# Two heads side by side on halves of the tensor array in float32, in place of one block-diagonal float32r product per pair of heads

## The chip, the cores and the metric

One core of a Trainium2 chip runs the kernel: TensorE for matrix products (PE, with PEld for the loading of its weights), VectorE (DVE), ScalarE (ACT), GpSimd (POOL), and SyncE (SP), which issues the DMAs. The metric is the device time of one execution in microseconds; lower is better. Float32r is a float32 format of which TensorE uses fewer bits in a product, and float32 is its full format, which the trace shows as two PE instructions for one product.

## The reference

A linear attention with a decaying state, and then a gated MLP over its output (4 batches, 8 heads, 768 tokens, 48 values a head; 384 channels, hidden size 1536):

```python
for t in range(S):
    kt, vt, rt = (k[:, :, t], v[:, :, t], r[:, :, t])
    cur = np.einsum('bhd,bhe->bhde', u[None] * kt, vt)
    y[:, :, t] = np.einsum('bhd,bhde->bhe', rt, state + cur)
    state = w[None, :, :, None] * state + np.einsum('bhd,bhe->bhde', kt, vt)
...
x = np.ascontiguousarray(attn_out.transpose(0, 2, 1, 3)).reshape(B, S, H * D)
xt = x.transpose(0, 2, 1)
h = xt @ U @ V
u = x + h.transpose(0, 2, 1)
ch = np.maximum(u @ w_ch1, 0.0) @ w_ch2
return (u + ch).astype(np.float32)
```

`w_ch1`, `w_ch2`, `U` and `V` arrive as float64, whose bits the kernel turns into float32 itself.

## The kernel before

The attention goes by chunks of 128 tokens, numbered `n` from 0 to 23, six to a batch. Tables of powers of w turn the decay into plain products within a chunk. Heads are taken in four pairs (`NP`), and a pair's 2 x 48 = 96 values (`PD`) lie on 96 partitions. For a chunk:

- `a_pre` makes on POOL `ks` (k scaled, for the state) and `dv` (the diagonal term; its sum over a head's values, `dg`, is DVE's).
- `a_tr_r` and `a_tr_k` give r and k with values on partitions, scaled by the tables (`rT`, `kT`). For chunks 0 to 5 PE transposes; from chunk 6 on DVE transposes 32 x 32 blocks (`bl`) that small DMAs bring from memory, and POOL multiplies by the table.
- The scores of the two heads of a pair come from one product: `kT` of the pair holds both heads on 96 partitions, and r is laid out block-diagonally, 128 columns with the first head's rows only and 128 with the second's. `bm`, a mask by partition, makes these halves. From chunk 6 on r and k are split into float32r high and low parts (`rh`, `rl`, `kh`, `kl`, on ACT and DVE), and three float32r products per pair (lines 388 to 390) make up one of nearly full precision. Chunks 0 to 5 (`plain`) use one float32 product per pair (line 383).
- `am`, the causal mask on the scores, is DVE's (three times ACT's and POOL's).
- `a_sq` reads the state: `rT` of a pair times `S`, whose 96 x 96 blocks are block-diagonal (line 410). `a_av` adds `am` times v, head by head (line 421), in the same PSUM bank (`pav`). `x` is that plus `dv` (line 430).
- `a_su` makes the state's update, `ks` of a pair times v of the pair, of which the two diagonal blocks count (line 449), and DVE and POOL form the next `S` (lines 457 and 458).

The MLP of a batch (`m_1`, `m_2`) is made of 48 steps over halves of the tokens and blocks of the hidden size; each step has 9 float32r products of 384 columns in `m_1` (lines 613 to 615) and 9 in `m_2` (631 to 633), with a ReLU and a split on ACT and DVE between them (`hh`, `hl`). The program runs the first batch's attention together with the conversion of the first 12 units of weights (`raw_w`, three DVE operations each, then ACT and POOL: the first stage), and then for each batch its MLP with the next batch's attention spread over it. A scheduler with a timeline of its own sets the order of instructions on each engine; each engine then works through its list in order. `queued` holds some weight conversions behind given steps.

Eight PSUM banks are shared by tags: `tr`, `sc`, `av` one each, `mm` two, `acc` three.

Of the kernel before, what the change touches and what calls it, by code (L numbers as in the profile page):

```python
# [23 lines left out]
def rwkv_moe(ctx: ExitStack, tc: tile.TileContext, r, k, v, w, u, U, V, w1, w2, out):  # L24
# [5 lines left out]
    PD = 2 * D  # L30
# [21 lines left out]
    def f32(ap):  # L52
        return ap.bitcast(F32)

# [7 lines left out]
    bm = const.tile([PD, 2, D], F32, name="bm")  # L62
    nc.gpsimd.memset(bm, 1.0)
    nc.gpsimd.affine_select(out=bm[:, 0, :], in_=bm[:, 0, :], pattern=[[0, D]], compare_op=ALU.is_gt,
                            fill=0.0, base=D, channel_multiplier=-1)
    nc.gpsimd.affine_select(out=bm[:, 1, :], in_=bm[:, 1, :], pattern=[[0, D]], compare_op=ALU.is_ge,
                            fill=0.0, base=-D, channel_multiplier=1)
# [11 lines left out]
    nc.sync.dma_start(wT[:, :, 0], w.rearrange("(q j) d -> (j d) q", j=2))  # L79
    ub = const.tile([128, H, D], F32, name="ub")  # L80

    def tables():
        """Powers of w by products of its repeated squares, and of their inverses."""
# [23 lines left out]
        for x_, t in ((1, tab), (0, tabr)):  # L107
            pt = ps_tile("tr", f"pt_tab{x_}", 1)
            for q in range(NP):
                nc.tensor.transpose(pt[:, q * PD:(q + 1) * PD], tabT[:, x_, q, :], ident[:PD, :PD])  # L110
            nc.scalar.copy(t, pt[:, :DM])
        w2p = const.tile([PD, NP, 1], F32, name="w2p")
        nc.vector.tensor_mul(w2p, top[0], top[0])
        nc.gpsimd.tensor_mul(wm, bm.rearrange("p j e -> p (j e)").unsqueeze(1).broadcast_to([PD, NP, PD]),
                             w2p.broadcast_to([PD, NP, PD]))

    def flags():
        """Whether any of w lies where the tables cannot serve."""
# [11 lines left out]
    wm = const.tile([PD, NP, PD], F32, name="wm")  # L130
# [4 lines left out]
    # One pool of equal slots: a unit of weights as it arrives, its two halves for the rest of the program,  # L135
    # and later the blocks of r and k.
# [27 lines left out]
    def unit(name, shape, parts, split):  # L164
        """Loads an array of float32 or of float64 (as its bits); gives float32 to be split into float32r halves."""
# [70 lines left out]
    NB = B * NCH  # L236
    loaded = {}
    pre = {}
# [11 lines left out]
    def a_load(n):  # L250
        b, c = divmod(n, NCH)
        ts = []
        if n < 4:
            t3 = xpool.tile([128, 3, H, D], F32, tag="uTl" if n % 2 else "uTh", name=f"ld_{n}", bufs=2)
            ts = [t3[:, i] for i in range(3)]
            for t, src in zip(ts, (r, k, v)):
                nc.sync.dma_start(t, src[b, :, c * C:(c + 1) * C, :].rearrange("h p d -> p h d"))
            loaded[n] = ts
            return
        for nm, src in (("r", r), ("k", k), ("v", v)):  # L260
            t = work.tile([128, H, D], F32, tag="ldv" if nm == "v" else "ldrk", name=f"ld{nm}_{n}", bufs=3 if nm == "v" else NRK)
# [4 lines left out]
    def a_load_blocks(n, i, q):  # L266
        # partitions 32 g + tt, free (pair, token block, i): 32 x 32 blocks of three chunks' tokens by (head, dim)
        b, c = divmod(n, NCH)
        if q == 0:
            bls[n, i] = big([PD, 2, 12, 32], F32, f"bl_{n}_{i}")  # L270
        t = bls[n, i]
        src = (r, k)[i % 2]
        for g, i0, j, d0, ln in ((0, 0, 0, 0, 32), (1, 0, 0, 32, 16), (1, 16, 1, 0, 16), (2, 0, 1, 16, 32)):
            sv = src[b, 2 * (2 * (i // 2) + q) + j, c * C:(c + 3) * C, d0:d0 + ln].rearrange("(m t) d -> t m d", t=32)
            nc.sync.dma_start(t[32 * g:32 * g + 32, q, :, i0:i0 + ln], sv)  # L275
# [3 lines left out]
    def fl(t):  # L279
        return t.rearrange("p h d -> p (h d)")  # L280
# [622 lines left out]
```

## Time and profile before

| | us |
|---|---|
| median of 3 runs | 495.33 (494.27 to 496.04) |
| the profiled execution, first to last instruction | 492.1 |
| PE busy | 461.5 |
| DVE busy | 303.3 |
| POOL busy | 235.6 |
| ACT busy | 149.6 |
| first MLP product starts at | 76.2 |

The profile is of one execution; the median of the runs is 3.2 us above its span. Busy time of PE counts overlapping instructions once, and its matmuls are pipelined, so a busy PE is not a PE at its best pace: that is read from the distances between the starts of its instructions. What ends an idle stretch is given behind an arrow with its line. All times in tables of stretches are counted from the span's start.

### The profile page before, as it was taken

The page shows a single profiled execution, that of the slowest core. Times are in us where ns is not written, and L with a number is a line of the kernel's source. Part 1 is how long each engine was busy: PE and PEld are TensorE (multiplying, and loading weights), DVE is VectorE, ACT ScalarE, POOL GpSimd, SP SyncE. Part 2 cuts the span into 40 slices and gives each one's busy share as a digit, 9 for nine tenths or more (in the row PEclk, how much of TensorE's full clock was granted, in tenths as well). Part 3 has the DMA queues.
Part 4 walks back from the last instruction along what each step waited for, and adds up shares of the span by engine and source line. Part 5 has one row for each costly group of instructions (what it writes and reads, how often), then busy time and mean ns, then how long its engine had stood idle before and what let it go on. Part 6 is the DMA issues. An engine that isn't in the chain of part 4 may idle for free.

```text
span 492.1 us, 7932 instructions
## 1 busy us (share of the span) xinstructions
PE 461.5 (94%) x2891; PEld 446.6 (91%) x2891; DVE 303.3 (62%) x543; ACT 149.6 (30%) x290; POOL 235.6 (48%) x227
## 2 busy tenths in 40 slices
PE   7869878979999999999999999999999999999994
PEld 6858757969998989999999999999999999999994
DVE  7998968997788666837677453676672533213112
ACT  3535524434332232333222322323231222211110
POOL 5957565747978571645777602468751021000000
PEclk9977969999999999999999999999999999999998
DMA  9999704554764663676267225542001152001001
GB/s 159 200 312 405 160 17 73 89 82 74 103 113 95 101 102 90 152 107 97 50 96 140 54 66 108 107 75 50 2 0 49 57 113 73 0 1 48 1 0 55
DMA packets 196880, 45.23 MB, mean 92 GB/s; under 512 B 187682, under 2 KB 193571, under 8 KB 196835
## 3 DMA queue, kind: packets, MB, share of 16 engines
q1 hardware_dynamic: 196834, 44.66, 44.2%
q8 instruction: 25, 0.41, 0.4%
q14 instruction: 21, 0.16, 0.1%
HBM read 35.79 MB, written 8.85 MB: 91 GB/s over the span
## 4 chain that ended last, share of the span: by engine, by line
PE 64%; DVE 14%; POOL 7%; issue 6%; SPq 4%; DMA 3%; ACT 1%; DVEq 0%; POOLq 0%; ACTq 0%
PE p L631 8%; PE p L632 8%; PE p L613 8%; PE p L633 8%; PE p L615 8%; PE p L614 8%; PE pav L421 5%; SPq L275 3%; DVE rl L353 2%; PE pav L410 2%; DVE raw_w L189 2%; POOL kT L323 2%; PE psu L449 2%; DVE raw_w L188 1%; POOL dv L295 1%
## 5 line engine op out<-in xcount | busy, mean ns | idle before, releaser
L619 DVE SCALAR_TENSOR_TENSOR hl<-p,hh 128x384 fp32r<-128x384 f32 x96 | 52.6, 549 | 102.1 <-ACT hh L618 102.0
L613 PE MATMUL p<-uTh,w1s 128*128 128x384 f32 x288 | 98.3, 344 | 2.8 <-DVE hl L619 2.5
L631 PE MATMUL p<-w2s,hh 128*128 128x384 f32 x288 | 98.5, 342 | 1.4 <-ACT hh L618 1.4
L614 PE MATMUL p<-uTl,w1s 128*128 128x384 f32 x288 | 97.7, 339 | 1.2 <-DVE uTl L546 1.2
L615 PE MATMUL p<-uTh,w1s 128*128 128x384 f32 x288 | 97.3, 338 | 0.0
L632 PE MATMUL p<-w2s,hh 128*128 128x384 f32 x288 | 96.7, 336 | 0.0
L618 ACT ACTIVATE hh<-p 128x384 fp32r<-128x384 f32 x96 | 46.7, 489 | 148.5 <-PE p L615 147.3
L633 PE MATMUL p<-w2s,hl 128*128 128x384 f32 x288 | 78.8, 338 | 0.1
L613 PEld LDWEIGHTS p<-uTh,w1s 128*128 128x128 f32 x288 | 54.4, 189 | 4.6 <-DVE hl L619 3.7
L631 PEld LDWEIGHTS p<-w2s,hh 128*128 128x128 f32 x288 | 54.2, 188 | 2.6 <-ACT hh L618 2.4
L614 PEld LDWEIGHTS p<-uTl,w1s 128*128 128x128 f32 x288 | 54.6, 190 | 2.0 <-DVE uTl L546 2.0
L615 PEld LDWEIGHTS p<-uTh,w1s 128*128 128x128 f32 x288 | 54.5, 189 | 0.0
L632 PEld LDWEIGHTS p<-w2s,hh 128*128 128x128 f32 x288 | 54.2, 188 | 0.0
L601 POOL TENSOR_TENSOR uTl<-ut,uTh 128x384 fp32r<-128x384 f32 x21 | 21.5, 1025 | 66.6 <-ACT uTh L600 65.2
L633 PEld LDWEIGHTS p<-w2s,hl 128*128 128x128 f32 x288 | 52.5, 189 | 0.5 <-DVE hl L619 0.2
L323 POOL TENSOR_TENSOR kT<-kT,tabT 96x512 f32<-96x512 f32 x18 | 27.3, 1518 | 42.0 <-DVE kT L321 32.7
L421 PEld LDWEIGHTS pav<-ldv,am 128*128 128x128 f32 x320 | 43.4, 198 | 1.5 <-DVE am L397 1.5
L421 PE MATMUL pav<-ldv,am 128*128 128x48 f32 x320 | 42.8, 272 | 0.6 <-DVE am L397 0.5
L397 DVE TENSOR_TENSOR am<-psc,mask 128x512 f32<-128x512 f32 x45 | 30.5, 678 | 9.7 <-PE psc L390 8.0
L353 DVE SCALAR_TENSOR_TENSOR rl<-rT,bm,rh 96x512 fp32r<-96x512 f32 x36 | 34.1, 959 | 3.9 <-ACT rh L351 3.9
L351 ACT ACTIVATE rh<-rT,bm 96x512 fp32r<-96x512 f32 x36 | 24.1, 716 | 22.8 <-POOL rT L323 22.6
L323 POOL TENSOR_TENSOR rT<-rT,tabT 96x512 f32<-96x512 f32 x18 | 24.8, 1379 | 10.8 <-DVE rT L321 10.7
(142 smaller groups left out, 766.6 us busy)
## 6 DMA issues: line engine op xcount, KB each, us to landing
raw_w<-in_moe_w_ch_dram SPq DMA_DIRECT2D x24, 384.0 KB, 7.8
out_dram<-x SPq DMA_DIRECT2D x24, 192.0 KB, 2.1
ud<-x SPq DMA_DIRECT2D x21, 192.0 KB, 2.0
ub<-ud SPq DMA_DIRECT2D x84, 48.0 KB, 2.3
ldr<-in_r_dram SPq DMA_DIRECT2D x20, 192.0 KB, 3.2
ldk<-in_k_dram SPq DMA_DIRECT2D x20, 192.0 KB, 4.0
ldv<-in_v_dram SPq DMA_DIRECT2D x20, 192.0 KB, 3.1
bl<-in_r_dram SPq DMA_DIRECT2D x48, 48.0 KB, 2.4
```

The lines of the kernel that those rows point to most:

```text
L323: nc.gpsimd.tensor_mul(xT, xT, tabT[:, i])
L353: nc.vector.scalar_tensor_tensor(rl[:, :, j, :], rT, bm[:, j, 0:1], f32(rh[:, :, j, :]), ALU.mult, ALU.subtract)
L397: nc.vector.tensor_tensor(am, pt.rearrange("p (h t) -> p h t", h=4), mask.unsqueeze(1).broadcast_to([128, 4, C]), ALU.mult)
L421: nc.tensor.matmul(avp[n][:, h * D:(h + 1) * D], lhsT=am[:, hh, :], rhs=vt[:, h, :], start=(c == 0 and h == 0), stop=(h == H - 1), skip_gr ...
L613: nc.tensor.matmul(pt, lhsT=wt[:, 0, fs], rhs=uh[:, ct, :], start=(ct == 0), stop=False)
L614: nc.tensor.matmul(pt, lhsT=wt[:, 0, fs], rhs=ul[:, ct, :], start=False, stop=False)
L615: nc.tensor.matmul(pt, lhsT=wt[:, 1, fs], rhs=uh[:, ct, :], start=False, stop=(ct == NCT - 1))
L618: i_hh = nc.scalar.activation(hh, pt, AF.Relu)
L619: i_hl = nc.vector.scalar_tensor_tensor(hl, pt, 0.0, f32(hh), ALU.max, ALU.subtract)
L631: nc.tensor.matmul(pt, lhsT=hh[:, ts_], rhs=W2[f][:, 0], start=(f == 0), stop=False)
L632: nc.tensor.matmul(pt, lhsT=hh[:, ts_], rhs=W2[f][:, 1], start=False, stop=False)
L633: nc.tensor.matmul(pt, lhsT=hl[:, ts_], rhs=W2[f][:, 0], start=False, stop=(f == NFT - 1))
```

## The change

Each head of a pair gets 64 partitions (`HP`), 48 of them used, so that the second head starts at partition 64. Scores are then two products per pair, one for each head, with 48 rows that lie in the upper or the lower half of the array (64 x 128); the state is kept as one 48 x 48 block per head at partitions 0 and 64, and its read is two products on these halves too. The update is two products whose 64 and 48 weight columns go to the left and the right half of the array (128 x 64). All of them are plain float32, for all chunks. `in_turn` fixes the order so that the halves alternate. `bm`, the block-diagonal layouts and the splits into high and low parts are gone.

```diff
-    PD = 2 * D
+    HP = 64
+    PD = HP + D
+    PE_ = 2 * HP
...
-        if plain(n):
-            rf = work.tile([PD, NP, 2, C], F32, tag="bd_rl" if odd else "bd_r", name=f"rf_{n}", bufs=1)
-            for j in range(2):
-                nc.scalar.activation(rf[:, :, j, :], rT, AF.Copy, scale=bm[:, j, 0:1])
...
-        for j in range(2):
-            nc.scalar.activation(rh[:, :, j, :], rT, AF.Copy, scale=bm[:, j, 0:1])
-        for j in range(2):
-            nc.vector.scalar_tensor_tensor(rl[:, :, j, :], rT, bm[:, j, 0:1], f32(rh[:, :, j, :]),
-                                           ALU.mult, ALU.subtract)
+        rT = work.tile([PE_, NP, C], F32, tag="rT", name=f"rT_{n}", bufs=2)
+        a_tr(n, 0, rT)
+        trs[n] = [rT]
...
-        nc.scalar.copy(kh, kT)
-        nc.vector.tensor_tensor(kl, kT, f32(kh), ALU.subtract)
...
+    def in_turn(steps):
+        last = None
+        for f in steps:
+            with ExitStack() as st:
+                if last is not None:
+                    st.enter_context(tc.issue_after(last.ins))
+                last = f()
...
-            nc.tensor.matmul(o, lhsT=kh[:, q, :], rhs=a, start=True, stop=False)
-            nc.tensor.matmul(o, lhsT=kh[:, q, :], rhs=bb, start=False, stop=False)
-            nc.tensor.matmul(o, lhsT=kl[:, q, :], rhs=a, start=False, stop=True)
+        pts = [ps_tile(tag, f"psc_{n}_{j}", 1) for j, tag in enumerate(("sc", "tr"))]
+        def one(q, j):
+            rows = head_rows(j)
+            return nc.tensor.matmul(pts[j][:, q * C:(q + 1) * C], lhsT=kT[rows, q, :], rhs=rT[rows, q, :],
+                                    start=True, stop=True)
+        in_turn([lambda q=q, j=j: one(q, j) for q in range(NP) for j in range(2)])
...
+            avp[n] = [ps_tile("av", f"pav_{n}_0", 1), ps_tile("sc", f"pav_{n}_1", 1)]
+        def one(q, j):
+            rows = head_rows(j)
+            return nc.tensor.matmul(avp[n][j][:, q * D:(q + 1) * D], lhsT=rT[rows, q, :], rhs=St[n][rows, q, :],
+                                    start=(q == 0), stop=False, skip_group_check=True)
...
-            nc.tensor.matmul(pt[:PD, q * PD:(q + 1) * PD], lhsT=ks[:, q * PD:(q + 1) * PD],
-                             rhs=vt[:, 2 * q:2 * q + 2, :].rearrange("p h d -> p (h d)"),
+            m = D if j else HP
+            k0 = (2 * q + j) * (HP if n < NCH else D)
+            return nc.tensor.matmul(pt[j * HP:j * HP + m, q * D:(q + 1) * D],
+                                    lhsT=ks.rearrange("p h d -> p (h d)")[:, k0:k0 + m], rhs=vt[:, 2 * q + j, :],
```

Further edits: a half of the heads (even or odd, `j`) now has its own score bank (`sc`, `tr`) and its own output bank (`av`; for the other `sc` from chunk 6 on, `mm` before), so `x` is written in two halves; r, k and `ks` of the first batch are padded to 64 values a head by small memsets on DVE; w is loaded by two DMAs; the block DMAs bring 64 instead of 48 values a head (four DMAs as before); `wm`, `S` and the sum of the state have half the columns; the slow path for other w takes its two buffers elsewhere.

The scheduler gives another order. Names carry the chunk's number first (`psc_13_1` is chunk 13's scores, odd heads) and then a running number. PE around chunk 13, beside the third batch's MLP, before; the rows left out are the MLP's, and more of the score products:

```order
L388 MATMUL psc_13_1_2312<-rh_13_2194,kh_13_2225 128x256
L389 MATMUL psc_13_1_2312<-rl_13_2195,kh_13_2225 128x256
L390 MATMUL psc_13_1_2312<-rh_13_2194,kl_13_2226 128x256
...
L410 MATMUL pav_13_2342<-S_12_2252,rT_13_2190 128x96 x4
...
L421 MATMUL pav_13_2342<-ldv_13_1753,am_13_0_2310 128x48 x4
...
L421 MATMUL pav_13_2342<-ldv_13_1753,am_13_1_2319 128x48 x4
...
L388 MATMUL psc_14_0_2458<-rh_14_2351,kh_14_2395 128x256
```

The same place in the change:

```order
L411 MATMUL pav_13_0_2355<-S_12_2270,rT_13_2212 128x48
...
L379 MATMUL psc_13_0_2320<-rT_13_2212,kT_13_2243 128x128
L379 MATMUL psc_13_1_2321<-rT_13_2212,kT_13_2243 128x128
...
L411 MATMUL pav_13_1_2356<-S_12_2270,rT_13_2212 128x48
L411 MATMUL pav_13_0_2355<-S_12_2270,rT_13_2212 128x48
...
L424 MATMUL pav_13_0_2355<-ldv_13_1786,am_13_0_2330 128x48 x4
L461 MATMUL psu_13_2413<-ldv_13_1786,ks_13_2183 64x48
L461 MATMUL psu_13_2413<-ldv_13_1786,ks_13_2183 48x48
...
L424 MATMUL pav_13_1_2356<-ldv_13_1786,am_13_1_2332 128x48 x4
...
L379 MATMUL psc_14_0_2471<-rT_14_2365,kT_14_2409 128x128
```

The eight scores now stand together, then 23 MLP products, then the rest of the state's read, both `pav` groups and the update in one piece, then 23 MLP products up to the next chunk's scores; only one product of the read stands apart, near the scores.

POOL at the end of the first stage, before: the states after chunks 3 and 4 (`S_3`, `S_4`), a mask's select, and weights (`w1s`, `w2s`).

```order
L458 TENSOR_TENSOR S_3_548<-S_3_548,wm_86 96x384
L394 AFFINE_SELECT am_4_0_567<-am_4_0_567 128x512
L201 TENSOR_TENSOR w2s_1_555<-raw_w2_1_234,w2s_1_555 128x384
L201 TENSOR_TENSOR w2s_2_589<-raw_w2_2_236,w2s_2_589 128x384
L458 TENSOR_TENSOR S_4_623<-S_4_623,wm_86 96x384
```

In the change:

```order
L471 TENSOR_TENSOR S_3_594<-S_3_594,wm_83 112x192
L311 TENSOR_TENSOR ks_6_964<-ldk_6_831,tab_84 128x384
L314 TENSOR_TENSOR dv_6_966<-ldr_6_829,ldk_6_831 128x384
L317 TENSOR_TENSOR dv_6_966<-dv_6_966,ub_80 128x384
L389 AFFINE_SELECT am_4_0_619<-am_4_0_619 128x512
L320 TENSOR_TENSOR dv_6_966<-ldv_6_833,dg_6_969 128x384
L311 TENSOR_TENSOR ks_7_1061<-ldk_7_837,tab_84 128x384
L314 TENSOR_TENSOR dv_7_1063<-ldr_7_835,ldk_7_837 128x384
L317 TENSOR_TENSOR dv_7_1063<-dv_7_1063,ub_80 128x384
L471 TENSOR_TENSOR S_4_681<-S_4_681,wm_83 112x192
```

The weights of this place moved ahead of `S_3`, and what chunks 6 and 7 need from POOL, which in before follows the first stage, moved between the two states.

DVE at the same place, before: the masks and the outputs `x` of chunks 4 and 5, with the last steps of three weight units between.

```order
L430 TENSOR_TENSOR x_4_637<-pav_4_592,dv_4_503 128x384
L190 SCALAR_TENSOR_TENSOR raw_w2_3_244<-raw_w2_3_244 128x384
L397 TENSOR_TENSOR am_5_0_642<-psc_5_0_639,mask_72 128x512
L190 SCALAR_TENSOR_TENSOR raw_w2_4_246<-raw_w2_4_246 128x384
L397 TENSOR_TENSOR am_5_1_653<-psc_5_1_650,mask_72 128x512
L190 SCALAR_TENSOR_TENSOR raw_w2_5_248<-raw_w2_5_248 128x384
L430 TENSOR_TENSOR x_5_689<-pav_5_666,dv_5_578 128x384
```

In the change, from the last step of the same weight unit on:

```order
L191 SCALAR_TENSOR_TENSOR raw_w2_5_249<-raw_w2_5_249 128x384
L392 TENSOR_TENSOR am_3_0_533<-psc_3_0_523,mask_72 128x512
L392 TENSOR_TENSOR am_3_1_535<-psc_3_1_524,mask_72 128x512
L434 TENSOR_TENSOR x_3_576<-pav_3_0_555,dv_3_462 128x4x48
L470 TENSOR_TENSOR S_3_594<-psu_3_585,S_2_515 112x192
...
L392 TENSOR_TENSOR am_4_1_622<-psc_4_1_610,mask_72 128x512
L319 TENSOR_REDUCE dg_6_969<-dv_6_966 128x8
L319 TENSOR_REDUCE dg_7_1066<-dv_7_1063 128x8
L434 TENSOR_TENSOR x_4_663<-pav_4_0_642,dv_4_541 128x4x48
L470 TENSOR_TENSOR S_4_681<-psu_4_672,S_3_594 112x192
...
L434 TENSOR_TENSOR x_5_741<-pav_5_1_728,dv_5_628 128x4x48
```

The weight units of the first stage now stand ahead of chunk 3's masks, and the sums `dg` of chunks 6 and 7 ahead of the state after chunk 4.

More of the change, by code (lines that the diff above doesn't have):

```diff
@@ L393, in a_sc, with a_am @@
+    def a_am(n, j):
+        pt = scs[n][j]
+        am = work.tile([128, 4, C], F32, tag="am", name=f"am_{n}_{j}", bufs=2)
+        if n < NCH and (n * 2 + j) % 4 < 1:
             nc.scalar.copy(am, pt.rearrange("p (h t) -> p h t", h=4))
```

181 lines of the change are left out of this document (83 added, 98 removed).

## The prediction

> **What bounds the kernel now.** I read the page's busy shares first, then busy times by stretch, then PE's timeline.
>
> ```profile
> PE 461.5 (94%) x2891; PEld 446.6 (91%) x2891; DVE 303.3 (62%) x543; ACT 149.6 (30%) x290; POOL 235.6 (48%) x227
> 0.00:77.00 77.00, 62.29 (x362) 54.16 (x362) 64.71 (x115) 34.35 (x68) 53.20 (x62) 0.84 0.78 200
> 77.00:175.00 98.00, 90.67 (x578) 86.55 (x579) 80.34 (x140) 34.63 (x69) 67.90 (x61) 0.98 0.60 96
> 175.00:285.00 110.00, 108.18 (x712) 106.47 (x712) 72.47 (x134) 33.42 (x62) 64.61 (x60) 1.00 0.53 96
> 285.00:384.00 99.00, 99.00 (x661) 98.39 (x661) 56.62 (x102) 27.59 (x53) 43.78 (x40) 1.00 0.27 57
> 384.00:492.00 108.00, 101.37 (x585) 101.05 (x583) 29.16 (x55) 19.63 (x41) 6.10 (x6) 0.98 0.15 40
> ```
>
> The columns are the stretch, its length, the busy time of PE, PEld, DVE, ACT and POOL, and the granted clock, DMA share and GB/s. Until 77 us the first batch's attention and the first weights run, with DVE the fullest engine (64.7 of 77). From 77 us the MLPs run with the other batches' attention in between, and PE is the bound: 7.3 us idle until 175, 1.8 until 285, none after. So three things count: what the new products cost on PE, what waits disappear before 285 us, and whether the first stage gets longer.
>
> Busy time hides PE's pace, since matmuls overlap. The pace is the distance between starts:
>
> ```profile
> 326.00 0.84 PE L449 MATMUL psu<-ldv,ks 128*96 128x96 f32 x8
> 326.68 1.02 PE L421 MATMUL pav<-ldv,am 128*128 128x48 f32 x8
> 327.52 0.42 PE L613 MATMUL p<-uTh,w1s 128*128 128x384 f32 x1
> 327.78 0.34 PE L614 MATMUL p<-uTl,w1s 128*128 128x384 f32 x1
> 327.95 0.34 PE L615 MATMUL p<-uTh,w1s 128*128 128x384 f32 x1
> 328.13 0.34 PE L613 MATMUL p<-uTh,w1s 128*128 128x384 f32 x1
> ...
> 332.00 1.03 PE L410 MATMUL pav<-S,rT 96*128 96x96 f32 x8
> 332.81 0.42 PE L613 MATMUL p<-uTh,w1s 128*128 128x384 f32 x1
> ...
> 334.81 0.28 PE L388 MATMUL psc<-rh,kh 96*128 96x256 f32 x1
> 334.93 0.28 PE L389 MATMUL psc<-rl,kh 96*128 96x256 f32 x1
> ...
> 335.52 0.99 PE L421 MATMUL pav<-ldv,am 128*128 128x48 f32 x8
> 24.19 1.96 PE L383 MATMUL psc<-rf,kf 96*128 96x256 f32 x8
> 25.99 0.60 PE L312 MATMUL ptr<-ident,ld 128*96 128x128 f32 x4
> ```
>
> An MLP product takes 0.174. The six score products from 334.81 to 335.52 take 0.118 each. Every float32 product is two PE instructions (x8 for four products): the state's read (L410) takes 0.81/8 = 0.101 each with 96 columns moving, the scores' times v (L421) 0.84/8 = 0.105 with only 48. So the moving side does not set this pace; it does at 256 columns (L383, first batch: 1.80/8 = 0.225), so that 128 columns cost at most 0.113, and I take 0.107. The update (L449), 96 weight columns instead of 128, takes 0.68/8 = 0.085: the pace goes with the weights' columns. The Trainium skill ("TensorE: Matmul & The Clock Gate", LDWEIGHTS) gives columns/1.2 ns, 107 for 128 and 80 for 96, and the trace agrees. And the MLP product behind a float32 group starts 0.26 before its successor instead of 0.174: leaving such a group costs 0.085.
>
> PE from 76.2 to 485.0 is 408.8 us. 1728 MLP products at 0.1735 are 299.8; 216 score products at 0.119 25.7; 15 state reads at 0.81 12.2; 36 halves of L421 at 0.84 30.2; 15 updates at 0.68 10.2; about 60 exits at 0.085 5.1; 36 G products 6.3 and 23 gate products 4.1 at 0.175. That is 393.6, so some 15 us are waits. The ends, and the PE waits that the profile names before 175 us:
>
> ```profile
> 76.21 0.44 PE L613 MATMUL p<-uTh,w1s 128*128 128x384 f32 x1
> 485.05 1.49 DVE L636 TENSOR_TENSOR x<-p,x 128x384 f32<-128x384 f32 x3 [1.69 <-PE p L633]
> PE p L613 <- DVE hl L619: 2.2, 2, 1.6
> PE psc L389 <- DVE rl L353: 1.6, 2, 1.2
> PE ph L524 <- DVE x L525: 1.5, 1, 1.5
> PE p L631 <- ACT hh L618: 1.4, 2, 0.9
> ```
>
> **The change on PE, per chunk beside an MLP.** Everything becomes float32 with 128 weight columns, except the update. Scores: 12 products become 8 (16 instructions, N=128). State read: 4 become 8 (16 instructions, N=48). L421 stays at 16. Update: 4 become 8, 16 instructions of 64 and 48 columns; from 0.105 at 128 and 0.085 at 96 the line gives about 0.065 and 0.055. No row of before shows products on halves of the array, so both ends are bounded. *Side by side*, a pair costs one: scores 8 x 0.107 = 0.86, state read 1.05 (its first product stands alone, behind the scores, then seven in four slots of 0.21), update about 0.5. *One after the other*: 1.71, 1.68, 0.95. Over 18 chunks (15 for read and update), before 25.7 + 12.2 + 10.2 = 48.1; side by side 15.4 + 15.8 + 7.5 = 38.7, or 9.4 less; one after the other 30.8 + 25.2 + 14.3 = 70.3, or 22 more. I take the first end: the halves have their own rows, or their own columns, of the array, and the order alternates them. Nothing measured here excludes the other.
>
> Between full array and halves there are some seven changes per chunk (into the scores and out, into the read, to L421, to the update, to L421, out), against some 3.5 float32 exits before. I price each like the only exit the trace has, 0.085: 18 x 3.5 x 0.085 = 5.4 more. Bounds: nothing, and 0.2 each (+20). The Trainium skill ("TensorEngine Tiling (Array Packing)", Key Properties) says that changing the tiling mode drains the engine; it gives no time and no run here shows it. PE's net: -9.4 + 5.4 = **-4**, between -15 and +11.
>
> **DVE, ACT, POOL.**
>
> ```profile
> L353 DVE SCALAR_TENSOR_TENSOR rl<-rT,bm,rh 96x512 fp32r<-96x512 f32 x36 | 34.1, 959 | 3.9 <-ACT rh L351 3.9
> L372 DVE TENSOR_TENSOR kl<-kT,kh 96x512 fp32r<-96x512 f32 x18 | 20.8, 1155 | 0.0
> L351 ACT ACTIVATE rh<-rT,bm 96x512 fp32r<-96x512 f32 x36 | 24.1, 716 | 22.8 <-POOL rT L323 22.6
> L371 ACT CAST kh<-kT 96x512 fp32r<-96x512 f32 x18 | 11.2, 620 | 32.9 <-PE psc L389 18.2 <-POOL kT L323 7.0 <-POOL rT L323 2.9
> L430 DVE TENSOR_TENSOR x<-pav,dv 128x384 f32<-128x384 f32 x24 | 13.1, 546 | 6.4 <-PE pav L421 6.4
> L397 DVE TENSOR_TENSOR am<-psc,mask 128x512 f32<-128x512 f32 x45 | 30.5, 678 | 9.7 <-PE psc L390 8.0 <-PE psc L383 1.3
> L149 DVE MEMSET Uf<- 128x204 f32 x1 | 0.2, 228 | 0.0
> L301 POOL TENSOR_TENSOR dv<-ldv,dg 128x384 f32<-128x384 f32 x18 | 15.4, 853 | 9.1 <-DVE dg L300 9.1
> L394 POOL TENSOR_SCALAR_AFFINE_SELECT am<-am 128x512 f32<-128x512 f32 x3 | 2.0, 673 | 0.0
> ```
>
> DVE loses 34.1 + 20.8 = 55 us. x in two halves: from 546 ns for 384 elements and 678 for 512, about 1.03 ns each, so 0.35 a half, 24 x 0.15 = +3.6; the state's sum on half the columns gives about as much back. Twelve memsets of the pad columns: 0.28 for 256 and 0.15 for 128 elements by L149's row, 2.3 us, mostly while DVE waits for its first data. ACT loses 24.1 + 11.2 and the plain chunks' rf; POOL's product with wm halves. On the path this is worth only part of the 15 us of waits, since PE never waits after 285 us. DVE's share until 175 us falls from 80.3 by some 18 (six chunks at 3.1); I take **-10**, between -4 and -15. What is late next there is POOL, 67.9 of 98 us, which the change relieves of half a product a chunk only. DMA: as many block loads and packets, a third more bytes in them; hidden, the DMA share there is 0.6. wT comes in two DMAs, an issue more at the head of SP's queue, which DVE meets behind its memsets. Transposes on PE and DVE cover 128 partitions instead of 96 with the same elements in each, and cost the same.
>
> The new bank rule: the second output half takes the score bank, so it waits for the first mask product (0.68), and the next chunk's scores wait for x. In PE's order some 20 MLP products, 3.5 us, stand at both places, so it is hidden; without that cover it would be about 1 us a chunk.
>
> **The first stage.** Its order moves most. In before, three weight units' last steps stand between chunk 5's masks, and the end looks like this:
>
> ```profile
> 65.46 0.68 DVE L397 TENSOR_TENSOR am<-psc,mask 128x512 f32<-128x512 f32 x1
> 66.06 0.77 DVE L190 SCALAR_TENSOR_TENSOR raw_w<-raw_w 128x384 int32<-128x384 int32 x1
> 68.81 0.56 DVE L430 TENSOR_TENSOR x<-pav,dv 128x384 f32<-128x384 f32 x1 [1.98 <-PE pav L421]
> 72.96 1.00 POOL L292 TENSOR_TENSOR ks<-ldk,tab 128x384 f32<-128x384 f32 x1
> 73.91 1.00 POOL L295 TENSOR_TENSOR dv<-ldr,ldk 128x384 f32<-128x384 f32 x1
> 74.99 1.01 POOL L298 TENSOR_TENSOR dv<-dv,ub 128x384 f32<-128x384 f32 x1
> ```
>
> The weights end at 66.8, x of chunk 5 at 69.4; POOL prepares chunks 6 and 7 afterwards. In the change all twelve units stand ahead of chunk 3's masks, so they end earlier by the attention work they no longer wait between (five masks at 0.68, two sums and three x at about 0.55: 6.2, of which I count 5 for the new dg and halves): 62. But then chunks 3 to 5 are left, and on POOL six products of chunks 6 and 7 (1.0 each) and dv by dg (0.85) stand between the state after chunk 3 and the one after chunk 4, which chunk 5's read waits for; on DVE their two dg stand there too. From 62: masks, L421, update and sum 3.1; POOL 3 products, one select (0.65), the 0.85, 3 more, dg and the sum on DVE, the state's product: 9.5; then read and both L421 2.5 and x 0.4. That is 77.5 against 69.4: **+8**, between +3 (had POOL these done while it waits) and +13 (PE at half clock in the gaps, as it is granted 0.84 in this stage). What stands behind, from x to the first MLP product, stays 6.8.
>
> **Sum** against the profiled span of 492.1: -4 - 10 + 8 = -6, so 486. The median of the runs is 3.2 above that span: 489.
>
> **Rivals.** *One after the other.* The half products take turns on weight loading. For it: the pace of 0.105 goes with columns loaded, not with what is done with them; against it: that row has one product on the whole array. PE +22 + 5, waits -10, first stage +8: +25, 520. This is the side that loses; it decides as soon as a pair costs more than about 1.2 of a single one (0.2 x 38.7 = 8 us). The Trainium skill ("TensorEngine Tiling (Array Packing)", Instruction Overhead) warns against tiling a dimension that is already small, and the read's N goes to 48: the trace agrees that N=48 costs as much as 96, and by that alone the read would be in this rival.
>
> *Everything hides.* No price for the changes of mode, all 15 us of waits gone, first stage +3: -9.4 - 15 + 3 = -21, 474. For it: DVE loses 18 us where PE waits. Against: POOL, and the order of the first stage.
>
> *The gain is eaten.* Side by side, but changes at 0.2 or a first stage of +13: between 494 and 505.
>
> **Numbers.** Side by side with partial gain 0.53 (489, its own range 478 to 500), everything hides 0.09, eaten 0.10, one after the other 0.28. Under 0.3% (1.5 us) this measurement cannot tell a change. Of the first case 0.43 is faster beyond it, 0.05 the same and 0.05 slower; the second is faster; the third 0.02 faster, 0.02 the same, 0.06 slower; the fourth slower. Together 0.54 faster, 0.07 same, 0.39 slower. The range, 474 to 520, leaves out half of the fourth case and little else.
>
> **What the changed profile would show.** Score products of a pair (L379) starting within 0.02 to 0.03 of each other and eight instruction pairs in 0.86 us: step one right; sixteen at 0.107 in a row: the serial rival. MLP products behind the read, L421 and update at more than 0.26: dearer changes. PE idle from 85 to 175 us under 3: the waits gone. The first MLP product at 84 instead of 76.2, with POOL on ks and dv between two S products: the first stage. I am wrong if the halves share the weight path, or if DVE reaches chunk 3 well before 62.

## The result, and the profile after

The changed kernel takes 517.2 us (median; 512.8 to 522.4) beside 494.8 for the kernel before: 4.3% slower, ratio 1.043 (95% interval 1.037 to 1.049). The prediction said 489, with a range (474 to 520) that still held 517. The profiled execution has a span of 517.3 us against 492.1, 25.2 more. Here and below ratios leave out runs more than 1.5% above the fastest of their kernel, and medians are of all runs.

Busy times from the page, then the same stretches as before, but for the first cut, which moves with the first MLP product:

```profile
PE 484.9 (94%) x3331; PEld 451.8 (87%) x3331; DVE 253.4 (49%) x525; ACT 109.4 (21%) x224; POOL 219.4 (42%) x224
0.00:96.00 96.00, 77.14 (x487) 64.40 (x488) 66.16 (x133) 26.16 (x53) 55.11 (x62) 0.64 0.76 169
96.00:175.00 79.00, 72.35 (x521) 66.70 (x521) 52.34 (x110) 22.37 (x48) 50.56 (x48) 0.96 0.62 102
175.00:285.00 110.00, 110.00 (x842) 102.90 (x839) 53.76 (x118) 19.09 (x39) 58.19 (x59) 1.00 0.61 109
285.00:384.00 99.00, 99.00 (x720) 93.28 (x719) 43.52 (x93) 18.21 (x38) 46.85 (x47) 1.00 0.33 65
```

DVE and ACT fell by 50 and 40 us as foreseen, and PE rose by 23. The first stage runs at a mean clock of 0.64. It is the loss: in steps of 10 us (clock third from the end of a row), with PE's and DVE's timeline around it,

```profile
50.00:60.00 10.00, 5.12 (x31) 4.09 (x29) 10.00 (x18) 3.94 (x9) 5.81 (x5) 0.50 0.93 221
60.00:70.00 10.00, 10.00 (x62) 8.46 (x62) 4.43 (x8) 2.37 (x6) 6.92 (x7) 0.50 0.01 2
70.00:80.00 10.00, 10.00 (x59) 8.22 (x59) 2.42 (x5) 1.75 (x3) 5.19 (x7) 0.50 0.57 98
80.00:90.00 10.00, 10.00 (x68) 8.56 (x68) 2.00 (x4) 0.00 (x0) 0.83 (x1) 0.65 0.10 20
60.32 1.84 DVE L191 SCALAR_TENSOR_TENSOR raw_w<-raw_w 128x384 int32<-128x384 int32 x2
62.08 1.27 DVE L392 TENSOR_TENSOR am<-psc,mask 128x512 f32<-128x512 f32 x2
59.98 1.54 PE L480 MATMUL pG<-x,Uf 128*66 128x384 f32 x2 [1.25 <-DVE x L434]
92.02 3.70 PE L77 MATMUL p_wake<-ident 128*128 128x128 f32 x24
96.47 0.44 PE L626 MATMUL p<-uTh,w1s 128*128 128x384 f32 x1
```

the weights end at 62 as predicted and chunk 3's masks come behind them. But from 60 on it is PE that has hardly any idle time, for 32 us and at half clock for most of them; DVE and POOL wait for it. The first MLP product starts at 96.5 instead of 76.2: **20.3 of the 25.2 us**.

Beside the MLP, PE's timeline of one chunk:

```profile
348.39 1.09 PE L411 MATMUL pav<-S,rT 48*128 48x48 f32 x14
349.40 1.09 PE L424 MATMUL pav<-ldv,am 128*128 128x48 f32 x8
350.43 0.67 PE L461 MATMUL psu<-ldv,ks 128*64 128x48 f32 x16
351.02 1.09 PE L424 MATMUL pav<-ldv,am 128*128 128x48 f32 x8
351.94 0.42 PE L627 MATMUL p<-uTl,w1s 128*128 128x384 f32 x1
...
355.61 1.16 PE L379 MATMUL psc<-rT,kT 48*128 48x128 f32 x16
356.61 0.32 PE L411 MATMUL pav<-S,rT 48*128 48x48 f32 x2
356.86 0.39 PE L495 MATMUL pG<-xh,Us 128*66 128x384 f32 x1
```

Sixteen score instructions take 1.00 us from start to start of what follows: the halves do run side by side (within a pair the starts are 0.006 to 0.007 apart, pairs 0.107 to 0.111). Adding up, for every PE instruction from the first MLP product on, the time to the start of the next one (the last two columns are the runs e12_first_as_changed and e9_both_stages below):

| us, by kind | before | changed | e12 | e9 |
|---|---|---|---|---|
| MLP products, with the waits among them | 317.1 | 319.1 | 316.8 | 316.8 |
| scores | 28.2 | 20.0 | 20.7 | 20.7 |
| state's read | 12.1 | 19.4 | 12.9 | 12.9 |
| scores times v | 29.3 | 33.0 | 28.9 | 29.0 |
| update | 10.4 | 9.2 | 11.6 | 11.6 |
| G and gate products | 11.8 | 12.8 | 11.0 | 11.1 |
| sum | 408.8 | 413.6 | 401.9 | 402.1 |

Scores give 8.2, read and scores times v take 11.1. And the waits that were to go are there again (96 to 175 us; total in us, how often, longest):

```profile
PE p L626 <- DVE hl L632: 3.1, 1, 3.1
PE pG L495 <- POOL xl L446: 1.6, 1, 1.6
PE p L627 <- DVE uTl L559: 1.2, 2, 1.0
```

### The profile page after: what moved, and what is told of

Same layout as the page of the kernel before. It is cut to its first block, busy times and chain, and to the rows that moved or that the text cites. A ratio compares the mean times of both kernels' runs of the same rounds, so it can differ in the third digit from the quotient of the medians.

```text
span 517.3 us, 8753 instructions
## 1 busy us (share of the span) xinstructions
PE 484.9 (94%) x3331; PEld 451.8 (87%) x3331; DVE 253.4 (49%) x525; ACT 109.4 (21%) x224; POOL 219.4 (42%) x224
## 4 chain that ended last, share of the span: by engine, by line
PE 80%; DVE 9%; SPq 4%; issue 2%; DMA 2%; ACT 1%; POOL 0%; DVEq 0%; ACTq 0%
PE p L644 10%; PE p L626 9%; PE p L646 9%; PE p L628 9%; PE p L645 9%; PE p L627 9%; PE pav L424 8%; PE psc L379 5%; PE pav L411 4%; PE psu L461 2%; SPq L290 2%; DVE raw_w L189 2%; DVE raw_w L190 2%; SPq L260 2%; DVE raw_w L191 1%
## 5 line engine op out<-in xcount | busy, mean ns | idle before, releaser
L646 PE MATMUL p<-w2s,hl 128*128 128x384 f32 x288 | 81.0, 339 | 0.0
L424 PEld LDWEIGHTS pav<-ldv,am 128*128 128x128 f32 x320 | 41.1, 198 | 1.4
L411 PEld LDWEIGHTS pav<-S,rT 48*128 48x128 f32 x320 | 28.7, 216 | 11.7 <-issue 9.5
L392 DVE TENSOR_TENSOR am<-psc,mask 128x512 f32<-128x512 f32 x45 | 29.1, 683 | 17.6 <-PE psc L379 17.6
L342 POOL TENSOR_TENSOR rT<-rT,tabT 112x512 f32<-112x512 f32 x18 | 23.6, 1313 | 32.0 <-DVE rT L340 30.0
L379 PE MATMUL psc<-rT,kT 48*128 48x128 f32 x384 | 33.9, 312 | 2.5 <-ACT kT L344 2.1
L379 PEld LDWEIGHTS psc<-rT,kT 48*128 48x128 f32 x384 | 28.0, 210 | 8.6 <-issue 4.0
```

Of the source, the lines that this page charges most:

```text
L379: return nc.tensor.matmul(pts[j][:, q * C:(q + 1) * C], lhsT=kT[rows, q, :], rhs=rT[rows, q, :], start=True, stop=True)
L392: nc.vector.tensor_tensor(am, pt.rearrange("p (h t) -> p h t", h=4), mask.unsqueeze(1).broadcast_to([128, 4, C]), ALU.mult)
L411: return nc.tensor.matmul(avp[n][j][:, q * D:(q + 1) * D], lhsT=rT[rows, q, :], rhs=St[n][rows, q, :], start=(q == 0), stop=False, skip_gr ...
L424: nc.tensor.matmul(avp[n][j][:, q * D:(q + 1) * D], lhsT=am[:, q, :], rhs=vt[:, h, :], start=(c == 0 and q == 0), stop=(q == NP - 1), skip ...
L646: nc.tensor.matmul(pt, lhsT=hl[:, ts_], rhs=W2[f][:, 0], start=False, stop=(f == NFT - 1))
```

## The experiments

Each is compared with the kernel before, run on the same chip; times are medians, and the diffs are shortened.

**Do the halves overlap because they alternate?** (`e1_apart`)

```diff
-in_turn([lambda q=q, j=j: one(q, j) for q in range(NP) for j in range(2)])
+in_turn([lambda q=q, j=j: one(q, j) for j in range(2) for q in range(NP)])
```

> The three groups on halves (scores, state's read, update) are issued head by head: four products of the lower half, then four of the upper, instead of alternating. Nothing else is changed. Theory (the alternation is what lets two heads share the array, and the loss lies elsewhere): products of one half start 0.107 us apart, a chunk's scores take about 1.6 to 1.7 us instead of 0.86, read and update likewise; beside the MLPs that is 18 x 0.8 + 15 x 0.8 + 15 x 0.4 = 32 us more, some of it made up by waits, so 535 to 550 us. Rival (the queue overlaps halves whatever the order, or the overlap is worth nothing): within 3 us of the changed kernel's 517.

547.1 us, ratio 1.103 (1.096 to 1.111), 30 us more than with alternation. A chunk's scores now start one by one:

```profile
367.39 1.34 PE L379 MATMUL psc<-rT,kT 48*128 48x128 f32 x13
368.47 0.31 PE L411 MATMUL pav<-S,rT 48*128 48x48 f32 x1
368.57 0.27 PE L379 MATMUL psc<-rT,kT 48*128 48x128 f32 x1
...
368.80 0.27 PE L379 MATMUL psc<-rT,kT 48*128 48x128 f32 x1
```

From the first start to the last it is 1.4 us. Within a half the starts are 0.11 apart; two products fall within one 0.11 only at the seam between lower and upper scores, and where the last scores (upper half) meet the first reads (lower half, L411). The overlap is real and is the order's doing.

**Clock or order, first tries.** `e2_warm` and `e6_fill_free` fill PE's idle time with products that nothing reads; `e3_weights_behind` restores an order by hand.

```diff
+    for _ in range(38):                      # e6: 46, into free columns of gps[0]
+        with tc.issue_after(last.ins):
+            last = nc.tensor.matmul(avp[2][0][:, 256:384], lhsT=ident, rhs=ident, start=False, ...)
```
```diff
-    merge(attn_units(0), [f for _, f in wu[:NW0]])
+    held = [f for _, f in wu[:6]]
+    held += [lambda f=f: queued(f, mark[0]) for _, f in wu[6:NW0]]   # mark: DVE's latest am, x or S
+    merge(attn_units(0), held)
```

> 38 products of the identity with itself (128 weight columns, 128 moving, float32), which nothing reads, stand on PE behind chunk 2's last product of scores times v, from about 47.5 to 60 us, where PE of the changed kernel waits for DVE and ACT with gaps of 1 to 2.6 us. Theory 1 (half clock: from 60 us on PE is the bound and runs at 0.50, since it was never busy long enough): the clock is at 1.00 from about 60 us, the 26 us of PE work between 60 and 86 shrink by some 13, the first MLP product starts at 82 to 86 instead of 96.5, total 503 to 507. Theory 2 (the order of DVE and POOL sets the end of the stage): the clock rises but PE waits instead; first MLP product at 94 to 97, total 514 to 518. Theory 3 (small products on half of the array let the clock fall again): clock up for the fill only, then 0.50 again, 517 to 521.

> The first stage's weight units from the seventh to the twelfth are queued on DVE behind the attention's latest DVE instruction at their place in the program (mask, x or state sum of chunks 2 to 5), and units 13 to 15 behind the last x of chunk 5, so that attention goes first again. Theory 2 (order): chunk 2's x comes at 47 instead of 55 us, PE has no 10 us of backlog at 60, first MLP product at 76 to 84, total 497 to 505. Theory 1 (half clock is the price): the chunks start earlier but PE's groups stay at half pace (eight instructions of scores times v in 1.94 us), so 3 chunks at about 9 us each: first MLP product at 84 to 90, total 504 to 511. If neither holds: 517.

> As in the run before with products of the identity, but 46 of them, written to a bank that no sum reads meanwhile, so that they can start at 47.5 us where PE waits, and not at 57. Theory 1 (half clock): PE is at full clock from about 53 us, the stretch from 60 us on takes the 20 us that it took at full clock there instead of 32, first MLP product at 83 to 88, total 503 to 509. Rival (what remains is the order of DVE's and POOL's work): first MLP product no earlier than the 91.0 of the run with the late fill, total 511 to 514.

All three lay outside the totals that their theories gave: 513.2, 515.8 and 516.4 us in the order of the texts above (ratios 1.041, 1.043, 1.044, intervals about 0.006 each way). The fill of `e2_warm` had to wait for x of chunk 2, since it shared a bank with it:

```profile
57.07 10.40 PE L403 MATMUL pav<-ident 128*128 128x128 f32 x76 [3.75 <-DVE x L442]
67.31 0.81 PE L488 MATMUL pG<-x,Uf 128*66 128x384 f32 x2
87.42 2.84 PE L77 MATMUL p_wake<-ident 128*128 128x128 f32 x24
91.01 0.44 PE L634 MATMUL p<-uTh,w1s 128*128 128x384 f32 x1
```

But it shows the price of the clock: the work that took 32.0 us from 59.98 on takes 20.1 here, at 0.97 to 1.00. So of 20.3 us lost about 12 hang on the clock, given this order. In `e6_fill_free` the clock was 0.92 from 50 to 60 us, 1.00 in the next ten and fell again, 0.61 from 70 to 80; the first MLP product was at 91.1. `e3_weights_behind` started it at 88.6, with the clock at 0.50 until 70 us and at 0.66 in the next ten, and lost 5 us again behind it (the MLP products with their waits, summed as in the table, took 324.8 us in place of 319.1).

**What brings the clock up?** A tail of products behind the changed kernel's last output add (`e4_tail`, `e11_tail2`), each kind after a rest.

```diff
+    rest(6, *full(48, 128)); rest(6, *half(48, 48)); rest(6, *full(48, 48)); rest(6, *half(48, 128))
+    rest(6, *full(24, 256, 96)); rest(6, *half(48, 48, (0,)))
+    pts = full(96, 128)
+    for i in range(12): half(4, 48, pts=both); full(4, 48, pts=both)
```

> The changed kernel with a tail behind its last output add, whose results nothing reads: six runs of one kind of float32 product each, every run after some 5 us of rest on PE: 48 on the full array with 128 columns moving; 48 pairs on halves with 48 moving; 48 on the full array with 48; 48 pairs on halves with 128; 24 of 96 rows with 256; 48 on one half alone with 48. Each is about 20 us long at half clock. Last, 96 full products, and then twelve times four pairs on halves and four full products, to price the change of mode. The tail adds 150 to 200 us. Theory A (what matters for the clock is how much of the array works): full products bring the clock up within 4 to 12 us of their start, halves with 48 columns stay at half pace for all of their 20 us. Theory B (only unbroken work matters): every kind comes up after the same time. Price of a change: a block of four pairs and four full products takes 1.71 us without any, 1.9 at 0.09 each, 2.1 at 0.2 each.

> The changed kernel with another tail behind its last output add, whose results nothing reads; every run of products after some 6 us of rest on PE. 48 products each on the full array with 64, 80, 96 and (fifth) 112 columns moving; fourth, 48 pairs on halves with 96; sixth, six times four products with 48 and four with 128; seventh, 48 with 128. Last, without rest, 96 products with 128, then 48 with 96, then 48 with 64. Theory A (the clock comes up where the columns moving fill more than some share of the 128 that an instruction takes): a threshold between 48 and 96, below it 20.7 us for 48 products, above it 13 to 15 us, halves like the full array, the mixture (88 on the mean) like 80 to 96; and behind full clock 64 falls back if it did not come up from rest. Rival (48 alone is special, by its size on chip): 64 comes up too. If 96 does not come up, the run with twice the columns has another cause than A. The tail adds about 220 us.

PE's timeline of the first tail and then of the second (`t_p` is the tail's output, `t_g` both operands). A slot is the place of one instruction, or of a pair side by side; 96 slots take about 20.5 us at half clock, and 10.7 at full clock, so a run that takes 13 or 14 us has brought the clock up on its way:

```profile
516.76 12.94 PE L900 MATMUL t_p<-t_g 128*128 128x128 f32 x96 [5.77 <-DVE t_g L895]
536.08 20.72 PE L908 MATMUL t_p<-t_g 48*128 48x48 f32 x192 [6.37 <-DVE t_g L895]
563.42 20.69 PE L900 MATMUL t_p<-t_g 128*128 128x48 f32 x96 [6.63 <-DVE t_g L895]
590.48 13.60 PE L908 MATMUL t_p<-t_g 48*128 48x128 f32 x192 [6.37 <-DVE t_g L895]
...
680.75 1.09 PE L908 MATMUL t_p<-t_g 48*128 48x48 f32 x16
681.77 1.09 PE L900 MATMUL t_p<-t_g 128*128 128x48 f32 x8
682.80 1.09 PE L908 MATMUL t_p<-t_g 48*128 48x48 f32 x16
683.82 1.12 PE L900 MATMUL t_p<-t_g 128*128 128x48 f32 x8
684.88 1.95 PE L908 MATMUL t_p<-t_g 48*128 48x48 f32 x16
```
```profile
543.43 20.74 PE L900 MATMUL t_p<-t_g 128*128 128x80 f32 x96 [6.37 <-DVE t_g L895]
570.54 13.92 PE L900 MATMUL t_p<-t_g 128*128 128x96 f32 x96 [6.37 <-DVE t_g L895]
590.83 20.80 PE L908 MATMUL t_p<-t_g 48*128 48x96 f32 x192 [6.37 <-DVE t_g L895]
```

Halves are not what matters (48 columns fail on the full array too, and pairs with 128 succeed); nor is unbroken work, since 20.7 us of it do not bring the clock up. Columns moving behind each set of weights do: 80 on the full array fail, 96 succeed; pairs of 48 rows fail with 96 and succeed with 128. Theory A had halves like the full array, and there it missed. A change between halves and the full array costs 0.13 us: 2.05 for a block of sixteen slots and two changes, where the pace of 0.1115 inside the blocks gives 1.78. And four us of such blocks took the clock down from 1.00 to 0.50.

**Twice the columns in the kernel, and what that changed besides.** `e7_twice_the_columns`:

```diff
-nc.tensor.matmul(avp[n][j][:, q * D:(q + 1) * D], lhsT=am[:, q, :], rhs=vt[:, h, :], ...)
+nc.tensor.matmul(put(n, j, q), lhsT=am[:, q, :], rhs=moving(n, vt[:, h, :]), ...)   # two copies, n < NCH
```

> In the first stage alone the state's read and the scores times v move each 48 columns twice (96 instead of 48), the second copy into columns of the bank that nothing reads. Nothing else is changed; PE has more to do and no less. Theory A (the clock follows the share of the time in which columns move; 48 behind 128 weight columns are too few): with 96 an instruction takes no longer at the same clock, and the clock comes up well before 86 us: first MLP product at 82 to 92, total 503 to 513. Rival (what counts is unbroken work, or 96 are still too few): clock 0.50 until 86 us as in the changed kernel, first MLP product at 96 to 98, total 516 to 519.

507.1 us (1.027; 1.025 to 1.029), inside theory A's range, and the first MLP product at 77.4. That looked like the proof for the clock, but the scheduler reckons with longer products and had given another order as well. So both halves of that change alone:

> The run with twice the columns changed two things: with the longer products in its reckoning the scheduler also put DVE's and POOL's work of the first stage in another order (masks and x of chunks 1 to 5 earlier among the weights' steps). This kernel has that run's instructions in that run's order on every engine, with the state's read and the scores times v of the first stage back to 48 columns moving. Theory clock (the columns make the difference): the first MLP product is at 90 to 98 as in the changed kernel (96.5), total 511 to 518. Theory order (the columns did nothing, the order everything): 76 to 79, 505 to 508. Both at once: between, 81 to 90.

> The counterpart: the changed kernel's instructions in the changed kernel's order on every engine, with 96 columns moving in the first stage's state read and scores times v (the second copy goes to columns of the bank that nothing reads). Theory clock: the clock comes up well before 86 us and the first MLP product is at 77 to 86, total 503 to 511. Theory order: 95 to 98, total 515 to 519. Both at once: 84 to 93.

(For both the columns were set after the order was.) The new order with 48 columns: 508.3 us, 1.028 (1.021 to 1.035), the first product at 80.3. The old order with 96: 520.1 us, 1.056 (1.049 to 1.063), and 88.9 in its profile. Its four runs lie far apart, at 511.4 (the profiled one), 518.8, 521.4 and 524.5 us; by the first two, which alone lie within 1.5% of the fastest, the ratio would be 1.043.

```profile
47.31 0.68 DVE L394 TENSOR_TENSOR am<-psc,mask 128x512 f32<-128x512 f32 x1
48.38 0.68 DVE L394 TENSOR_TENSOR am<-psc,mask 128x512 f32<-128x512 f32 x1
59.77 0.68 DVE L394 TENSOR_TENSOR am<-psc,mask 128x512 f32<-128x512 f32 x1
69.42 0.67 DVE L394 TENSOR_TENSOR am<-psc,mask 128x512 f32<-128x512 f32 x1
80.30 0.44 PE L643 MATMUL p<-uTh,w1s 128*128 128x384 f32 x1
```

These are DVE's masks of chunks 3, 4 and 5 and the first MLP product with the new order and 48 columns: chunk 3's at 47 to 49, not at 62. For the new order theory order comes closest (76 to 79 us for the first product, 505 to 508 in total). For the old order the total is nearest to that theory too, but the first product lies where both causes at once had it (84 to 93). The order alone moves the first product by 16 us (48 columns) or 11.5 (96), and the time by 9, or by 8 to 13 given those four runs; part is lost again behind it, as the MLP products with their waits took 324.4 us in the new order with 48 columns and 319.1 in the changed kernel. The columns move the first product by 3 to 8 us, as the clock comes up sooner, and gain nothing in time that the runs show. With the new order PE's slow pace lies beside DVE's conversions (from 60 to 70 us the clock is 0.50 and DVE is busy throughout); with the old one it comes behind them.

**The groups one by one.** `e5_scores_only` puts read and update back on the full array; `e8_pairs_whole` issues the upper half of each pair of scores first.

```diff
-return nc.tensor.matmul(avp[n][j][...], lhsT=rT[rows, q, :], rhs=St[n][rows, q, :], ...)
+nc.tensor.matmul(avp[n][:, q * 2 * D:(q + 1) * 2 * D], lhsT=rT[:PD, q, :], rhs=St[n][:, q, :], ...)
```
```diff
-in_turn([lambda q=q, j=j: one(q, j) for q in range(NP) for j in range(2)])     # a_sc alone
+in_turn([lambda q=q, j=j: one(q, j) for q in range(NP) for j in (1, 0)])
```

> Only the scores keep the halves. The state's read and update go back to the full array, two heads block-diagonal in float32 (96 columns moving; S and wm hold both blocks again, with zeros beside them), the output of a chunk is in one bank again and x is one sum. Theory (the read gains nothing on halves, 12.1 against 19.4 us beside the MLPs, and each change of mode costs 0.17): from the first MLP product to the end the changed kernel's 420.8 us lose 7.3 on the read and 3.8 on scores times v, and get back 1.2 on the update: 411, five less than before. The first stage, with 96 columns moving in read and update, is at full clock sooner: first MLP product at 80 to 90 instead of 96.5. Total 491 to 501. Rival (the read's loss is only the place of the waits): the stretch stays at 418 to 421, total 498 to 517.

> The kernel with the halves in the scores only, and one thing changed: of each pair of scores the product of the upper half is issued first. Its output bank is the one that comes free last, so that no first product can run ahead of its group: in the run before it stood alone, some products of the MLP ahead of the other seven, and the scores beside the MLPs took 25.6 us instead of the changed kernel's 20.0. Theory: 5.5 us less, of them all on PE: 492 to 495. Rival (PE's time there is filled from the waits that follow): 497 to 500.

499.1 us (1.011; 1.009 to 1.013), then 494.0 (0.999; 0.997 to 1.002). The first total lies in the ranges of theory and rival both, and from the first MLP product (79.9) to the end it took 418.4 us, the rival's figure and not the theory's 411. The read and scores times v did come down, to 12.7 and 29.8 us, but the scores rose to 25.6, as their first product went ahead alone. In the second run they took 20.7, which is the 5 us, and the total is the theory's.

**The parts together**, and the fourth corner of the square (`e9_both_stages`, `e12_first_as_changed`, `e15_best_48`): first stage all on halves, later chunks only scores; 96 columns move in the first stage of `e9_both_stages` and 48 in that of the other two.

```diff
+    def a_sq(n):
+        (a_sq_first if n < NCH else a_sq_full)(n)      # a_av and a_su likewise
```

> The parts that did best put together: the first stage of the run with twice the columns (halves for all three groups, 96 columns moving, first MLP product at 77.4), and from chunk 6 on the run before this one (only the scores on halves, pairs whole). Theory (stages add): 77.4 and the stretch of 418.4 less 5.5, 490; range 487 to 493, a little faster than before. Rival (an earlier first product only meets weights that DVE hasn't converted: its waits for uTl and hl were 3.7 and 3.1 us in the run with twice the columns against 1.2 and 3.1 in the changed kernel): 493 to 497.

> The kernel that put the best parts together, with the first stage's products back to 48 columns: the fourth corner of a square (first stage with 48 or 96 columns; later chunks all on halves or only the scores). The other corners are 517.2 (48, all halves), 507.1 (96, all halves) and 491.5 (96, only scores). Theory (both causes stand by themselves): the first MLP product is back at 94 to 97, the later chunks keep what they saved, 517.2 less 15.6 is 501.6; range 497 to 505. Rival (what the later chunks save is only the start of the MLP meeting converted weights): 508 to 517.

> The kernel that put the best parts together (491.5), in its own order on every engine, with 48 columns moving in its first stage again. Against the square's fourth corner (511.4, also 48 columns and only the scores on halves later) it differs in the order alone. Theory order (the first stage's loss is the order, the clock adds a few us to it): first MLP product at 78 to 84, total 491 to 497. Theory columns: 86 to 100, total 499 to 511.

`e9_both_stages`: 491.5 us, ratio 0.993 (0.990 to 0.996), faster than before in the middle though not in every run: its twelve lie between 487.2 and 499.7, those of before between 492.1 and 496.1. `e12_first_as_changed`: 511.4 (1.035; 1.030 to 1.039), 6 above its theory's range and inside the rival's, but not for the rival's reason: the later chunks kept their gain (401.9 against 413.6), and its own order put the first MLP product at 99.6. `e15_best_48`, the best one's order with 48 columns: 491.5 (0.993; 0.990 to 0.996). So the order and not the columns makes this difference too. Its profile is of a longer run (498.4 us): the clock was 0.50 from 20 to 60 us, and the first product, at 87.9, missed the 78 to 84 foreseen. Six of its nine runs took 489.0 to 491.7 us, at a mean clock of 0.950 to 0.959 against 0.926, which would put the clock's price in this order at some 7 to 9 us. This is not shown: no profile of a shorter run tells where its first product lay.

**Is DVE's relief worth 10 us by itself?** `e10_before_no_low_halves`, on the kernel before:

```diff
-            nc.vector.scalar_tensor_tensor(rl[:, :, j, :], rT, bm[:, j, 0:1], f32(rh[:, :, j, :]), ...)
-        nc.vector.tensor_tensor(kl, kT, f32(kh), ALU.subtract)
+        # the products take rh and kh in place of rl and kl
```

> The kernel before, without DVE's two subtractions that make the low halves of r and k (rl, kl) beside the MLPs; the scores' products read the high halves in their place, so PE has the same products and DVE 55 us less. The low halves are left out of the scores by that. The prediction's term (DVE's relief takes 10 us of PE's waits, 4 to 15): 480 to 490. Rival (the waits hang on the weights' conversion at the MLP's start, not on the splits; only the 1.6 us in which scores waited for rl go): 491 to 494.

488.4 us, 0.988 (0.985 to 0.991): 5.9 us by the ratio, inside the prediction's 4 to 15 and not the rival's 491 to 494. MLP products with the waits among them took 313.0 us in place of 317.1. The relief is worth something in the order of before; the changed kernel did not get it.

## Why the prediction was wrong, step by step

- **Halves side by side**: right. Pairs start 0.11 apart (0.107 was taken; the readings 0.101 and 0.105 of before divide in a shorter last instruction, and within those groups too the starts are 0.111 apart); the rival *one after the other* is what `e1_apart` had to be made for. Scores: 10.3 less two changes of mode a chunk (3.1) was foreseen, 8.2 came.
- **Changes of mode**: taken at 0.085, measured at 0.13 in the tail. The Trainium skill ("TensorEngine Tiling (Array Packing)", Key Properties) says that a change drains the engine; 0.13 is what a change costs here. With them the state's read costs 7.3 more than before where 3.6 and its share of the changes were foreseen, and scores times v, between two changes, 3.8. PE came to 1.7 more by the four kinds, 2.7 with G, not 4 less: the sign of this term was wrong, its mechanism right. The Trainium skill's rule against tiling a dimension that is already small ("TensorEngine Tiling (Array Packing)", Instruction Overhead), which the prediction weighed for the read, agrees with this case: with read and update off the halves the read takes 12.9 us in place of 19.4, and the same stretch 401.9, 7 less than before.
- **Waits, -10**: failed. MLP products with the waits among them went up by 2.1. `e10_before_no_low_halves` shows 5.9 us for the relief alone; the prediction named POOL as what is late next there. In the changed kernel the longest wait, 3.1 us for hl at 122 us, lies where DVE has three steps of weights, 5 us, ahead of hl, in its timeline:

```profile
119.88 2.17 DVE L190 SCALAR_TENSOR_TENSOR raw_w<-raw_w 128x384 int32<-128x384 int32 x1
121.97 2.90 DVE L191 SCALAR_TENSOR_TENSOR raw_w<-raw_w 128x384 int32<-128x384 int32 x2
124.80 0.55 DVE L632 SCALAR_TENSOR_TENSOR hl<-p,hh 128x384 fp32r<-128x384 f32 x1
```

  What is late there is still DVE, and not by its order alone: the median of each of these two lines is 0.55 us, so three such steps would take 1.7 and not 5.1. POOL's products fill the time from 118.0 to 124.5 us, and from 80 us on no step of these lines that stands clear of POOL's products takes more than 0.56. Why the steps are long stays open; no run moved them alone.
- **First stage, +8**: the step that failed most: +20.3. Its order was foreseen (all units ahead of chunk 3's masks, weights ended at 62). What followed was reckoned as a chain over POOL, 15.5 us from 62 to chunk 5's x; it took 28.5. The working left out PE's own sum: the work left at 60 us is 20 us of PE at full clock and 32 at the half clock that it had. "PE at half clock in the gaps" had it in the gaps only, worth 5 more; it held with hardly a gap (0.45 us is the only one over 0.1 from 60 to 92). An estimate from `e2_warm`: at full clock this work would have ended at about 80 and the first MLP product started at about 84, which is the +8. So the part that failed is PE's pace behind 62 us, and the 12 us beyond the forecast are of the size that the clock costs in this order. The order of `e13_order_of_96` avoids most of both parts, with the first product at 80.3.
- **Sum**: 1.7 (the four kinds) + 1.0 (G) + 2.1 (MLP products) + 20.3 (first stage) = 25.1 of 25.2, in place of -4 - 10 + 8.
- **Rivals**: that the range still holds 517 is luck, since its upper end stands for *one after the other* (520), which did not happen; the nearest in kind was *the gain is eaten* by a longer first stage, priced 494 to 505.

## What to carry to other kernels

Where a scheduler orders the work by its own reckoning, an edit of products can move other engines' work by tens of us: before crediting a change (or an experiment) look at the order, and hold the order fixed when the edit is to be priced. For a stage that ends late, add up what each engine still has to do behind the late point at the pace it has there, and not only the longest chain. Put on halves of the array what was limited by rows and has 128 columns moving (the scores), and leave small groups on the full array, where each change of mode costs as much as a product's instruction.

## What was not expected of the hardware

The clock does not follow busy time alone. The Trainium skill ("TensorE: Matmul & The Clock Gate", Part 1: The HAM clock gate) has about 3.4 us of sustained work bring the full clock; here 20.7 us without a gap stayed at 0.50 when float32 products moved 80 columns or fewer on the full array, or 96 on pairs of halves, and 3.2 to 6.3 us sufficed with 96 to 128 on the full array. Once up it holds at less: 64 columns kept it at 1.00 for the 10.7 us tried, while blocks of 48 with changes of mode lost it after four. Several of the kernels here also scatter more, the changed one by 10 us, `e14_96_in_old_order` by 13 and `e15_best_48` by 17, where the kernel before scatters by 4. The mean clock on record goes with it: 0.943, 0.931, 0.920 and 0.911 for the 511.4, 518.8, 521.4 and 524.5 us of `e14_96_in_old_order`. Few columns alone are not the reason, since with 96 `e9_both_stages` scatters by 12.5 and `e7_twice_the_columns` by 1.4. That the threshold goes by rows times columns fits the kinds tried (up to 0.69 of full rows times 128 columns fail, the mixture of 48 and 128 among them; 0.75 and more succeed), but no run separated it from other rules.
